# No gate product in the last period, and the last product's second bank summed and stored by halves of columns

## The chip, the cores and the metric

The kernel runs on one core of one Trainium2 chip. The time is device microseconds of one execution, lower is better. TensorE (PE) multiplies into PSUM banks of 128 partitions by 512 fp32 columns; VectorE (DVE) and ScalarE (ACT) take results out of the banks; SyncE (SP) and ACT issue DMA transfers.

## The reference

Linear attention without softmax, an RMS norm per head, and a gated feed-forward layer, all in fp32:

```python
kv  = np.einsum('bhsd,bhse->bhde', k, v)            # 8 batches, 8 heads, 576 rows, 64 columns
o   = np.einsum('bhsd,bhde->bhse', q, kv)
x   = o / np.sqrt(np.mean(o * o, axis=-1, keepdims=True) + 1e-6) * g_norm
x   = x.transpose(0, 2, 1, 3).reshape(8 * 576, 512)  # 4608 tokens of 512
h   = x @ w_in                                       # 512 -> 2048
g   = h * erf(np.maximum(h, 0) + np.log1p(np.exp(-np.abs(h))))   # h * erf(softplus(h))
out = g @ w_out                                      # 2048 -> 512
```

## The kernel before

The 4608 tokens are worked in nine groups of 512. Groups 0 to 7 are the first 512 rows of each batch; the ninth holds the 64 rows left over of each of the eight batches. Of the 2048 hidden columns, `BATCH` = 4 blocks of 128 form a batch of work, and `NB` = 4 batches make a group. The order of all instructions is written out by hand; there is no scheduler behind it.

From the third group on, each fp32 product is made of three fp32r products of parts ("forms") of its operands, which run at one pass each. `product` is the helper: it takes two PSUM banks, `n_ps` and `m_ps`, in turn from six; eight matmuls (two forms by four contraction blocks) sum into `n_ps`, four (the third form) into `m_ps`, all 512 columns wide. `hidden` uses it for h, `result` for the output: `result(T, b, j, g, w)` computes the 128 token rows j of group T, batch b, and adds the two banks into the sum `es[j]` in SBUF. For batches after the first of a group these are two VectorE operations of 128x512: `add_scaled` (L440) of `n_ps` times a constant, then `add` (L445) of `m_ps`.

The loop over periods m runs one step longer than there are batches. In period m the engines compute h of batch m (four calls of `hidden`), its softplus and erf on ACT, and the output of batch m - 1 (four calls of `result`, j = 0 to 3). After some of the calls of `result`, VectorE multiplies h by erf(softplus(h)) in two halves of the token columns, the "gates" (L876, 128x1024 each, `due_halves` says which). Before the next output product the gates are cut into forms: ACT takes the upper part (L405), VectorE the other two (L408, L411).

The last period, m = `batches` = 36, has no h to compute: it holds only the four output products of batch 35. Batch 35 is the fourth of the ninth group, so after each `result` the finished rows are stored. The lines that say which gates are due:

```python
            if m == batches - 1:
                due_halves = (j,) if j < 2 else ()
            else:
                due_halves = range(2) if j == (2 if to_last else 1) else ()
```

In period 36 these give both halves after j = 1. They multiply batch 35's h by its s once more; the forms of batch 35 were cut before, and nothing reads this h again.

`store` (L535) writes a block of the ninth group as two transfers of 64 rows by 512 columns, 128 KB each, one issued by SP and one by ACT, since the two halves of the partitions belong to two batches. At the end SP waits for all transfers and the engines meet in a closing barrier.

Of the kernel before, what the change touches and what calls it, by code (L numbers as in the profile page):

```python
# [60 lines left out]
def kernel(  # L61
# [13 lines left out]
    DM, DF = moe_w_in.shape[0], moe_w_in.shape[1] // 2  # L75
    J = 4
    G = J * P
    R = S - G
# [74 lines left out]
    for i in range(2):  # L153
        nc.gpsimd.dma_start(
            out=g_col[i * D : i * D + D, :], in_=g_norm.rearrange("(d one) -> d one", one=1)
# [100 lines left out]
    def weights():  # L256

        w_next("split")
        w_next("join")
        w_next("load")  # L260
# [178 lines left out]
    def add_scaled(out_, ps, scale):  # L439
        nc.vector.scalar_tensor_tensor(  # L440
            out=out_, in0=ps, scalar=scale, in1=out_, op0=ALU.mult, op1=ALU.add
        )

    def add(out_, ps):
        nc.vector.tensor_tensor(out=out_, in0=ps, in1=out_, op=ALU.add)  # L445

    banks = [(ps_h, "h"), (ps_h, "h")] + [(ps_o, f"o{i}") for i in range(4)]

    def product(weights, moving, turns=True):


        n_ps, m_ps = (
            pool.tile([P, G], FP32, name=name, tag=tag)
            for name, (pool, tag) in zip(("n_ps", "m_ps"), banks[:2])
        )
        if turns:
            banks.extend(banks[:2])
            del banks[:2]
        for ps, forms in ((n_ps, (0, 1)), (m_ps, (2,))):
            for k in range(4):  # L460
                for form in forms:
                    nc.tensor.matmul(  # L462
                        ps,
                        lhsT=weights(form, k),
                        rhs=moving(form, k),
                        start=(form == forms[0] and k == 0),
                        stop=(form == forms[-1] and k == 3),
                    )
        return n_ps, m_ps
# [36 lines left out]
    def hidden(T, f, turns=True):  # L506

        w = w_now["in", f].pop(0).rearrange("p i (c f) -> p i c f", c=KC).bitcast(FP32R)
        x = x_forms[T]
        return product(lambda form, c: w[:, form, c], lambda form, c: x[form][:, c], turns)  # L510
# [14 lines left out]
                stop=last,  # L525
            )

    def store(T, j, e):
        if T < B:
            rows = out[T * S : T * S + G, :].rearrange("(p j) f -> p j f", j=J)  # L530
            nc.sync.dma_start(out=rows[:, j, :], in_=e)
            return
        for h, side in enumerate((nc.sync, nc.scalar)):
            first_row = (2 * j + h) * S + G
            side.dma_start(out=out[first_row : first_row + R, :], in_=e[h * R : h * R + R, :])  # L535

    es = {}

# [10 lines left out]
    def unit(name):  # L549
        return gate.tile([P, G], FP32, name=name, tag=name[0])  # L550
# [30 lines left out]
    first_batch, batches = FIRST * NB, NG * NB  # L581
# [5 lines left out]
    def load_parts(which, n):  # L587


        pool = w_out_p if which == "out" and len(w_seq["out"]) > BATCH else w_in_p  # L590
        for _ in range(n):
            if w_seq[which]:
                key = w_seq[which].pop(0)
                t = pool.tile([P, 3, G], FP32, name=f"w_{which}_parts", tag="w")
                nc.sync.dma_start(out=t, in_=w_kept[key])
                w_now.setdefault(key, []).append(t)
# [47 lines left out]
    for n in range(FIRST * FC + 1):  # L644
        T, f = divmod(n, FC)
        if n == FC:
# [6 lines left out]
            forms = late.tile([P, 3, KC, G], FP32R, name="x_forms0")  # L653
# [24 lines left out]
        if T == FIRST - 1 and f >= WHOLE:  # L678
            n_ps, m_ps = hidden(T, f, turns=False)
        elif T < FIRST:  # L680
# [10 lines left out]
            for i, c in blocks:  # L691
# [3 lines left out]
                    rhs=xT[T][:, c, :],  # L695
# [3 lines left out]
        if T < FIRST:  # L699
            if n == whole:  # L700
                old_h = acc.tile([P, BATCH, G], FP32, name="h", tag="e")
            h = hs[n] = old_h[:, n - whole] if n >= whole else unit("h_sb")
# [28 lines left out]
        if n >= LAG:  # L731
            T2, f2 = divmod(n - LAG, FC)
# [21 lines left out]
    def part(h, half):  # L754
        return h[:, :, half * 2 * P : half * 2 * P + 2 * P]

    def cut_upper(h, half):

        t = late_r.tile([P, 3, BATCH, 2 * P], FP32R, name=f"g_forms{half}")
        upper(part(h, half), t[:, 0])  # L760
        return t

    def cut_lower(h, half, t):
        lower(part(h, half), *(t[:, i] for i in range(3)))

    def result(T, b, j, g, w):

        ps = product(
            lambda form, f: g[j // 2][:, form, f, j % 2 * P : j % 2 * P + P],
            lambda form, f: w[f][:, form],  # L770
        )
        if b == 0:
            if j == 0:
                all_e = wide.tile([P, J, DM], FP32, name="e", tag="a")
                es.update((i, all_e[:, i]) for i in range(J))
            nc.vector.tensor_scalar(
                out=es[j], in0=ps[0], scalar1=SHIFT - 1.0, scalar2=None, op0=ALU.mult
            )
        else:
            add_scaled(es[j], ps[0], SHIFT - 1.0)  # L780
        add(es[j], ps[1])


    FETCH = ("", "in", "in", "out", "in", "out", "in", "out out")
# [2 lines left out]
    for m in range(first_batch, batches + 1):  # L787
        T, b = divmod(m, NB)
        todo = []
        if T + 1 < NG:  # L790
            todo = list(attention(T + 1, b))
            if b == 0:
                side = late_r if T % 2 == FIRST % 2 else late
                forms = side.tile([P, 3, KC, G], FP32R, name=f"x_forms{(T + 1) % 2}")
                x_forms[T + 1] = [forms[:, i] for i in range(3)]

        def piece():
            if todo:
                todo.pop(0)()


        places = (0, 2, 3, 5, 6, 8)
        if T + 1 == B:
            places = (0, 0, 0, 5, 6, 7)
            if b == NB - 1:


                places, todo[3] = (0, 0, 0, 4, 6, 7), partial(todo[3], table=False)
                todo[5] = partial(chain, todo[5], softplus_table)
        elif b == NB - 1:  # L810
            places = (0, 2, 3, 5, 6, 7)

        def pieces(place):
            while todo and places[-len(todo)] <= place:
                todo.pop(0)()

        def fetch(place):
            for which in FETCH[place].split():
                load_parts(which, 1)


        to_last = m == B * NB - 1
        pieces(0)
        g, done = g_next, len(g_next)
        g_next = []
        if m < batches:

            pool, tag = (acc, "e") if m % 2 else (wide, "b")
            h = pool.tile([P, BATCH, G], FP32, name="h", tag=tag)
            s = gate_r.tile([P, BATCH, G], FP32, name="s", tag="s")  # L830
        for i in range(BATCH):
            if m < batches:
                n_ps, m_ps = hidden(T, b * BATCH + i)
            fetch(i)

            def evacuate():
                nc.scalar.activation(h[:, i], n_ps, AF.Copy, scale=SHIFT - 1.0)  # L837
                add(h[:, i], m_ps)


            early_copy = i == 0 and m == B * NB
            if early_copy:
                evacuate()
            if i == 0:
                for half in range(done, 2):
                    g.append(cut_upper(old_h, half))
            if done <= i < 2:
                cut_lower(old_h, i, g[i])
            if m < batches:
                if not early_copy:  # L850
                    evacuate()
                nc.scalar.activation(s[:, i], h[:, i], AF.Softplus)  # L852
            pieces(i + 1)
        if m < batches:
            for i in range(2):
                nc.scalar.activation(part(s, i), part(s, i), AF.Erf)  # L856
            if len(todo) < 2:
                softplus_table()
        T2, b2 = divmod(m - 1, NB)
        w = [w_now["out", b2 * BATCH + f].pop(0).bitcast(FP32R) for f in range(BATCH)]  # L860
        for j in range(J):
            result(T2, b2, j, g, w)
            fetch(BATCH + j)
            if b2 == NB - 1:
                store(T2, j, es.pop(j))
            if j == 1 and m == batches - 1:
                cut_lower(h, 0, g_next[0])

            if m == batches - 1:
                due_halves = (j,) if j < 2 else ()  # L870
            else:
                due_halves = range(2) if j == (2 if to_last else 1) else ()
            if to_last:
                pieces(BATCH + 1 + j)
            for half in due_halves:
                nc.vector.tensor_tensor(  # L876
                    out=part(h, half), in0=part(h, half), in1=part(s, half), op=ALU.mult
                )
            if j == 0 and m == batches - 1:
                g_next.append(cut_upper(h, 0))  # L880
            pieces(BATCH + 1 + j)
        old_h = h
# [33 lines left out]
```

## Time and profile before

| | |
|---|---|
| median of 4 runs | 944.36 us |
| the runs | 943.32, 944.28, 944.47, 944.45 us |
| profiled execution | 943.32 us, span 941.5 us (1.8 us lie around the span) |
| TensorE busy | 925.0 us, 98% of the span, granted clock 1.00 |
| VectorE busy | 742.9 us, 79% |
| ScalarE busy | 615.4 us, 65% |
| last matmul ends | 935.68 us |
| last VectorE sum ends | 937.75 us |

The span runs from the first to the last instruction of the program in the profiled execution. All positions in time below are microseconds from its start. "SPq" and "ACTq" rows are DMA issues by SP and ACT: how long the issuing takes, not the transfer. A busy matmul row counts a matmul from its start to its modelled end, and matmuls overlap: twelve of one product start 0.227 us apart, while each lasts 0.39 us.

### The profile page before, as it was taken

The page shows a single profiled execution, that of the slowest core. Times are in us where ns is not written, and L with a number is a line of the kernel's source. Part 1 is how long each engine was busy: PE and PEld are TensorE (multiplying, and loading weights), DVE is VectorE, ACT ScalarE, POOL GpSimd, SP SyncE. Part 2 cuts the span into 40 slices and gives each one's busy share as a digit, 9 for nine tenths or more (in the row PEclk, how much of TensorE's full clock was granted, in tenths as well). Part 3 has the DMA queues.
Part 4 walks back from the last instruction along what each step waited for, and adds up shares of the span by engine and source line. Part 5 has one row for each costly group of instructions (what it writes and reads, how often), then busy time and mean ns, then how long its engine had stood idle before and what let it go on. Part 6 is the DMA issues. An engine that isn't in the chain of part 4 may idle for free.

```text
span 941.5 us, 11743 instructions
## 1 busy us (share of the span) xinstructions
PE 925.0 (98%) x4272; PEld 683.4 (73%) x4272; DVE 742.9 (79%) x1056; ACT 615.4 (65%) x825; POOL 2.4 (0%) x10
## 2 busy tenths in 40 slices
PE   6999999999999999999999999999999999999997
PEld 4344445666688888888888888888888888888886
DVE  3999858887677787788778888888887777787667
ACT  4898876776766666666666666666666666665551
POOL 1000000000000000000000000000000000000000
PEclk9999999999999999999999999999999999999999
DMA  9876406899699998998899889988896779778871
GB/s 264 280 202 202 146 1 240 315 352 335 219 363 345 309 314 269 322 309 293 286 288 312 293 298 309 315 301 296 282 338 259 265 248 350 285 281 291 352 261 46
DMA packets 111842, 259.78 MB, mean 276 GB/s; under 512 B 43864, under 2 KB 69544, under 8 KB 111784
## 3 DMA queue, kind: packets, MB, share of 16 engines
q1 hardware_dynamic: 110152, 256.73, 79.0%
q10 hardware_dynamic: 1568, 2.29, 0.8%
q8 instruction: 34, 0.56, 0.2%
q14 instruction: 24, 0.20, 0.1%
q0 software_dynamic: 64, 0.00, 0.0%
HBM read 224.40 MB, written 34.60 MB: 275 GB/s over the span
## 4 chain that ended last, share of the span: by engine, by line
PE 95%; DVE 3%; DMA 1%; ACT 1%; issue 0%; DVEq 0%
PE n_ps L462 46%; PE m_ps L462 23%; PE o_ps L520 10%; PE h_ps L692 6%; PE se_ps L325 3%; PE kv_ps L297 2%; PE qt_ps L319 2%; PE ms_ps L351 1%; PE ms_ps L347 1%; PE ms_ps L346 1%; PE kv_ps L324 1%; DMA q_sb<-in_q_dram 1%; DMA v_sb<-in_v_dram 1%; PE kv_ps L305 0%; DVE xT L378 0%; DVE qT L369 0%
## 5 line engine op out<-in xcount | busy, mean ns | idle before, releaser
L462 PE MATMUL n_ps<-x_forms,w_in_parts 128*128 128x512 f32 x896 | 232.6, 401 | 0.1
L462 PE MATMUL n_ps<-w_out_parts,g_forms 128*128 128x512 f32 x928 | 231.3, 391 | 0.0
L462 PEld LDWEIGHTS n_ps<-w_out_parts,g_forms 128*128 128x128 f32 x928 | 174.2, 188 | 38.4 <-issue 1.7
L462 PEld LDWEIGHTS n_ps<-x_forms,w_in_parts 128*128 128x128 f32 x896 | 166.8, 188 | 43.1 <-issue 9.1
L852 ACT ACTIVATE s<-h 128x512 f32<-128x512 f32 x112 | 71.0, 634 | 179.2 <-DVE h L445 179.2
L445 DVE TENSOR_TENSOR h<-m_ps,h 128x512 f32<-128x512 f32 x116 | 79.8, 688 | 59.8 <-ACT h L837 43.8
L462 PE MATMUL m_ps<-w_out_parts,g_forms 128*128 128x512 f32 x464 | 124.2, 389 | 0.0
L462 PE MATMUL m_ps<-x_forms,w_in_parts 128*128 128x512 f32 x448 | 120.0, 389 | 0.0
L520 PE MATMUL o_ps<-w_out_sb,h_sb 128*128 128x512 f32 x224 | 100.8, 593 | 0.3 <-DVE h_sb L642 0.3
L462 PEld LDWEIGHTS m_ps<-w_out_parts,g_forms 128*128 128x128 f32 x464 | 87.1, 188 | 18.0
L462 PEld LDWEIGHTS m_ps<-x_forms,w_in_parts 128*128 128x128 f32 x448 | 84.1, 188 | 17.6
L445 DVE TENSOR_TENSOR e<-m_ps,e 128x512 f32<-128x512 f32 x116 | 80.3, 692 | 18.2 <-PE m_ps L462 10.9
L440 DVE SCALAR_TENSOR_TENSOR e<-n_ps,e 128x512 f32<-128x512 f32 x88 | 60.4, 686 | 38.9 <-PE n_ps L462 38.9
L520 PEld LDWEIGHTS o_ps<-w_out_sb,h_sb 128*128 128x128 f32 x224 | 42.3, 190 | 48.9 <-issue 46.6
L411 DVE SCALAR_TENSOR_TENSOR g_forms<-g_forms 128x1024 fp32r<-128x1024 f32 x58 | 71.1, 1226 | 2.0
L408 DVE TENSOR_TENSOR g_forms<-h,g_forms 128x1024 fp32r<-128x1024 f32 x58 | 70.6, 1218 | 1.7 <-ACT g_forms L405 1.4
L876 DVE TENSOR_TENSOR h<-h,s 128x1024 f32<-128x1024 f32 x58 | 68.3, 1218 | 0.7 <-ACT s L856 0.7
L837 ACT ACTIVATE h<-n_ps 128x512 f32<-128x512 f32 x112 | 65.4, 584 | 3.4 <-PE n_ps L462 3.4
L405 ACT ACTIVATE g_forms<-h 128x1024 fp32r<-128x1024 f32 x58 | 58.9, 1059 | 12.1 <-PE m_ps L462 8.7
L692 PE MATMUL h_ps<-xT,w_in_sb 128*128 128x512 f32 x144 | 64.8, 594 | 0.7 <-DVE w_in_sb L240 0.6
L106 ACT ACT_TABLE_LOAD x44 | 56.5, 1283 | 0.7
L856 ACT ACTIVATE s<-s 128x1024 f32<-128x1024 f32 x56 | 56.3, 1053 | 0.3
(98 smaller groups left out, 1014.0 us busy)
## 6 DMA issues: line engine op xcount, KB each, us to landing
w_out_parts<-w_out SPq DMA_DIRECT2D x116, 768.0 KB
w_in_parts<-w_in SPq DMA_DIRECT2D x112, 768.0 KB
w_in<-w_new SPq DMA_DIRECT2D x16, 768.0 KB
q_sb<-in_q_dram SPq DMA_DIRECT2D x32, 256.0 KB
w_raw<-in_moe_w_out_dram SPq DMA_DIRECT2D x8, 1024.0 KB
out_dram<-e SPq DMA_DIRECT2D x32, 256.0 KB
k_sb<-in_k_dram SPq DMA_DIRECT2D x28, 287.5 KB
v_sb<-in_v_dram SPq DMA_DIRECT2D x28, 287.5 KB
```

What stands on the lines that cost most here:

```text
L106: nc.scalar.preload_act_table_set("softplus")
L405: nc.scalar.activation(high, x, AF.Copy, scale=1.0 + 2.0**-13)
L408: nc.vector.tensor_tensor(out=low, in0=x, in1=high.bitcast(FP32), op=ALU.subtract)
L411: nc.vector.scalar_tensor_tensor(out=both, in0=low.bitcast(FP32), scalar=SHIFT, in1=high.bitcast(FP32), op0=ALU.mult, op1=ALU.add,)
L440: nc.vector.scalar_tensor_tensor(out=out_, in0=ps, scalar=scale, in1=out_, op0=ALU.mult, op1=ALU.add)
L445: nc.vector.tensor_tensor(out=out_, in0=ps, in1=out_, op=ALU.add)
L462: nc.tensor.matmul(ps, lhsT=weights(form, k), rhs=moving(form, k), start=(form == forms[0] and k == 0), stop=(form == forms[-1] and k == 3),)
L520: nc.tensor.matmul(o_ps[j], lhsT=g[:, j * P : j * P + P], rhs=w_out_sb[:, f, :], start=(f == 0), stop=last,)
L692: nc.tensor.matmul(plain[i], lhsT=w_in_sb[:, c, i % FC * P : i % FC * P + P], rhs=xT[T][:, c, :], start=(c == 0), stop=(c == KC - 1),)
L837: nc.scalar.activation(h[:, i], n_ps, AF.Copy, scale=SHIFT - 1.0)
L852: nc.scalar.activation(s[:, i], h[:, i], AF.Softplus)
L876: nc.vector.tensor_tensor(out=part(h, half), in0=part(h, half), in1=part(s, half), op=ALU.mult)
```

## The change

Three edits that act only in the last period. `due_halves` is empty there, so the two L876 products of period 36 are gone. In the last product (m = 36, j = 3) the `m_ps` bank is computed by column halves: four matmuls of 256 columns for the left half, then four for the right, where there were four of 512. Its sum into `es[3]` is made by two VectorE operations of 128x256, and after each the half is stored by its own pair of transfers, 64 rows by 256 columns, where one pair of 64 rows by 512 columns was issued after the whole sum. The `n_ps` bank and its `add_scaled` stay whole.

```diff
-    def product(weights, moving, turns=True):
+    def product(weights, moving, turns=True, cuts=1):
...
-        for ps, forms in ((n_ps, (0, 1)), (m_ps, (2,))):
+        spans = [slice(i * G // cuts, (i + 1) * G // cuts) for i in range(cuts)]
+        for ps, forms, cols in [(n_ps, (0, 1), slice(0, G))] + [(m_ps, (2,), x) for x in spans]:
             for k in range(4):
                 for form in forms:
                     nc.tensor.matmul(
-                        ps,
+                        ps[:, cols],
                         lhsT=weights(form, k),
-                        rhs=moving(form, k),
+                        rhs=moving(form, k)[:, cols],
                         start=(form == forms[0] and k == 0),
                         stop=(form == forms[-1] and k == 3),
                     )
...
-    def store(T, j, e):
+    def store(T, j, e, cols=slice(0, DM)):
...
-            side.dma_start(out=out[first_row : first_row + R, :], in_=e[h * R : h * R + R, :])
+            side.dma_start(
+                out=out[first_row : first_row + R, cols], in_=e[h * R : h * R + R, cols]
+            )
...
-    def result(T, b, j, g, w):
+    def result(T, b, j, g, w, cuts=1):
...
+            cuts=cuts,
...
-        add(es[j], ps[1])
+        for i in range(cuts):
+            cols = slice(i * DM // cuts, (i + 1) * DM // cuts)
+            add(es[j][:, cols], ps[1][:, cols])
+            if cuts > 1:
+                store(T, j, es[j], cols)
...
-            result(T2, b2, j, g, w)
+            cuts = 2 if m == batches and j == J - 1 else 1
+            result(T2, b2, j, g, w, cuts)
             fetch(BATCH + j)
             if b2 == NB - 1:
-                store(T2, j, es.pop(j))
+                e = es.pop(j)
+                if cuts == 1:
+                    store(T2, j, e)
...
-            if m == batches - 1:
-                due_halves = (j,) if j < 2 else ()
+            if m >= batches - 1:
+                due_halves = (j,) if j < 2 and m < batches else ()
```

## The prediction

> **What bounds the kernel.** I read the page first, then the chain that ended last over the final 40 us, then the last 10 us as a timeline, and last the windows after the last arithmetic. Part 1 of the page says who is scarce:
>
> ```profile
> PE 925.0 (98%) x4272; PEld 683.4 (73%) x4272; DVE 742.9 (79%) x1056; ACT 615.4 (65%) x825; POOL 2.4 (0%) x10
> ```
>
> TensorE is busy 98% of the span; no edit off its path can gain anything in the body. The instruction lists of the two programs are the same on every engine up to the last period but for line and buffer numbers, so only what follows TensorE's last matmul can change. The chain of waits, its last pieces (start, us, what):
>
> ```profile
> 932.95 1.81 PE n_ps L462 x8
> 934.76 0.92 PE m_ps L462 x4
> 935.68 0.68 DVE e L445
> 936.36 0.61 DVE e L440
> 936.97 0.03 issue
> 937.00 0.02 DVEq L445
> 937.02 0.04 issue
> 937.06 0.69 DVE e L445
> ```
>
> TensorE is done at 935.68, and three VectorE operations still stand behind it, one of them for the product before the last. VectorE is late, and the timeline of the period says why:
>
> ```profile
> 932.01 0.69 DVE L445 TENSOR_TENSOR e<-m_ps,e 128x512 f32<-128x512 f32 x1
> ...
> 932.62 2.35 DVE L876 TENSOR_TENSOR h<-h,s 128x1024 f32<-128x1024 f32 x2
> ...
> 932.79 1.98 PE L462 MATMUL n_ps<-w_out_parts,g_forms 128*128 128x512 f32 x8
> ...
> 934.60 1.07 PE L462 MATMUL m_ps<-w_out_parts,g_forms 128*128 128x512 f32 x4
> 934.88 0.68 DVE L440 SCALAR_TENSOR_TENSOR e<-n_ps,e 128x512 f32<-128x512 f32 x1
> 935.67 0.69 DVE L445 TENSOR_TENSOR e<-m_ps,e 128x512 f32<-128x512 f32 x1
> 936.28 0.68 DVE L440 SCALAR_TENSOR_TENSOR e<-n_ps,e 128x512 f32<-128x512 f32 x1
> 937.06 0.69 DVE L445 TENSOR_TENSOR e<-m_ps,e 128x512 f32<-128x512 f32 x1
> ```
>
> The two L876 products sit between the sums of j=1 and j=2; the first matmul group of j=2 ended at 932.05 (930.07 + 1.98), so L440 of j=2 starts 2.8 us after its bank was full. Nothing reads what L876 writes here. After the last sum the stores remain (timeline of SP, then windows: last two columns are the share of the DMA engines and GB/s):
>
> ```profile
> 937.78 0.47 SPq L535 DMA_DIRECT2D out_dram<-e  x1
> ```
>
> ```profile
> 938.50:939.00 0.50, 0.00 (x0) 0.00 (x0) 0.00 (x0) 0.00 (x0) 0.00 (x0) 1.00 0.30 82
> 939.00:939.50 0.50, 0.00 (x0) 0.00 (x0) 0.00 (x0) 0.00 (x0) 0.00 (x0) 1.00 1.02 197
> 939.50:940.00 0.50, 0.00 (x0) 0.00 (x0) 0.00 (x0) 0.00 (x0) 0.00 (x0) 1.00 0.79 283
> 940.00:940.50 0.50, 0.00 (x0) 0.00 (x0) 0.00 (x0) 0.00 (x0) 0.00 (x0) 1.00 0.01 0
> ```
>
> The trace's packet records sharpen these windows: the last store pair's packets run from 938.90 to 940.06, so 1.12 us from issue to first packet, 1.16 us of packets for 256 KB, and 1.47 us from the last packet to the span's end at 941.53 (landing, SP's waits, the closing barrier).
>
> **The products that go.** Two instructions of 1.22 us, both wholly on the path. Without them L440 of j=2 follows L445 of j=1 at VectorE's usual distance, 0.61 us (935.67 to 936.28): 932.01 + 0.61 = 932.62, when its bank is full. L445 follows 0.79 later (934.88 to 935.67): 933.41 to 934.10, and its store moves from 936.39 to 934.13, so its packets (1.12 later, 1.16 long) are gone by 936.4, before the next store's. What is late next is no longer VectorE's queue but the banks of j=3. Its first bank is full at 932.79 + 1.98 = 934.77, L440 starts 0.04 later (as elsewhere in the trace: bank full at 915.72, L440 at 915.76), 934.81, and L445 could start at 935.60; its own bank is full at 935.67, so it starts at 935.71. Ending at 936.40 in one piece instead of 937.75, it would gain 1.35 us. That is less than the 2.35 removed, because VectorE now waits for TensorE.
>
> **The halved matmuls.** Four matmuls of 512 columns, one per 0.227 us (four starts from 934.60), become eight of 256, each with its own weight load. If width sets the distance, eight take 8 x 0.113 = 0.91 us, as now: cost nothing. A weight load lasts 0.188 us in its row, which would seem to forbid 0.113; but loads overlap. Where this kernel has short matmuls (L324, L325), loads follow each other faster than they last:
>
> ```profile
> 654.07 0.42 PEld L324 LDWEIGHTS kv_ps<-qT_last,bd_kv 128*128 128x128 f32 x2
> 654.41 0.30 PEld L325 LDWEIGHTS se_ps<-qT,bd_kv 128*128 128x128 f32 x2
> ```
>
> Two loads of 0.19 in 0.30 us: 0.11 apart. That is nearest in shape, so I take 0.113 and a bank full at 935.67 again. Bounds: nothing to 0.91 us (if each matmul kept 0.227); a gain has no source, since the columns streamed are the same.
>
> **The halved sum.** In the changed program's list only the first half's sum waits for PE, and it waits for the count after all eight matmuls; the second waits for nothing. So the first half starts at 935.71, not after four matmuls. No 256-column sum is in the trace: 512 columns take 0.692, 1024 take 1.22, so the straight line gives 0.427, and the next instruction starts 0.08 before the end reported (0.692 against 0.61). Halves: 935.71 to 936.14 and 936.05 to 936.48, 0.08 later than the whole sum; by the 64-column copies (0.216 each, L326) at least 0.2 each, by the 512-column row at most 0.69, or 937.01.
>
> The Trainium skill's page PSUM — Partial Sum Buffer, section "PSUM bank collisions raise a hardware error", says that TensorE may not write a bank while another engine reads it, other columns included, so guards go by bank. It speaks against this cut: by it the first half waits as the list shows; without it the first half could start at 935.60, and the whole change would gain about 0.1 us more. No run here shows a collision.
>
> **The halved store.** Each queue now issues twice for j=3, and the second issue stands behind the first on SP and on ACT. First: 936.14 + 0.03 = 936.17 (the 0.03 from 937.75 to 937.78), lasting 0.47, to 936.64. Second: its sum was ready at 936.48, so the queue is what holds it, 936.70 with 0.06 for the semaphore wait ahead of it. That semaphore is one that a store of j=0 last used, issued at 931.33 and long landed, so the wait itself costs nothing. Packets start 1.12 after issue: 937.29 and 937.82. Packets of 1,024 bytes take 46 ns (median of 2,048 in the trace, loads), of 2,048 bytes 84 ns; a half pair then takes 1.16 x 46/84 = 0.64 us: 937.29 to 937.93, and the second, queued behind it, to 938.57. Bound above: a packet takes as long whatever its size, 2.32 us in all, to 939.61. Bound below: the second pair is not held and takes 0.5 us, to 938.32. I take 938.57, since the 46 ns is a row of the same size.
>
> The Trainium skill's page DMA: Bandwidth & Descriptors, section "Anatomy of one DMA — SWDGE (gpsimd) path", gives a transfer about 2.0 us plus its bytes at 436 GB/s (another issuing path than this one). By that an estimate for a whole pair is 2.60 us from 936.43, to 939.03, and for the second half pair 2.30 from 936.70, to 939.00: halving the store is worth nothing. The trace has 2.28 from issue to last packet for the whole pair.
>
> By the rows alone, one whole store from 936.43 would end its packets at 936.43 + 1.12 + 1.16 = 938.71; halves end them at 938.57, less one more semaphore wait of 0.06 in SP's closing sequence. The halves are worth 0.08 us, the removed products 1.35.
>
> **Sum.** Last packet 940.06 to 938.57 is 1.49, less 0.06: 1.43 us. The profiled execution took 943.32 (span 941.53 and 1.79 around it): 941.89. It was the fastest of four; against the median of 944.36 I predict 942.93. 0.2% of the time is 1.89 us, about what a measurement of this kernel can tell from no change.
>
> **Rivals.**
> (a) *Halves cost what wholes cost.* Packets keep their time: last packet 939.61, gain 940.06 - 939.61 - 0.06 = 0.39; or matmuls keep 0.227 us: everything 0.91 later, gain 0.52. About 943.9. For: SP's own packets in the final stores mostly take 0.15 to 0.17 us, twice the median of their size, so size is not all. Against: the load spacing of 0.11 and the 46 ns.
> (b) *Slower: the second store of a queue is held until the first has landed.* SP's wait for the last whole pair ended at 940.44, 0.38 us after the last packet and 2.66 after the issue. Two in series from 936.17 end before 940.44 only if each takes under 2.14 us. With 1.12 + 0.64 + 0.38 = 2.14 it is even; with 2.66 each, 941.49, 1.05 us slower, 945.4. Against: before, j=1's store issued at 932.73 while j=0's packets were still running.
> (c) *More in the tail than the profile shows.* Three of four runs were 1 us longer than the profiled one; if they spend it in the stretch that is cut, up to 2.4 us goes: 942.0.
>
> **How the numbers follow.** Forecast 0.72, (a) 0.16, (b) 0.05, (c) 0.07. The bounds of the forecast alone give gains of 1.0 to 1.7 us, 942.7 to 943.4. Runs of before lie up to 1.04 from their median, so a median of a few runs may be half a microsecond off; that, (a) and (c) give 942.0 to 944.3. Faster by over 0.2% needs 0.46 us more than the forecast: two fifths of its 0.72 through that scatter, plus (c), 0.36. Slower by over 0.2% is (b) with scatter, 0.06. The rest, 0.58, is within.
>
> **What would show it.** Right: L440 of j=2 at about 932.6, VectorE idle before the last L445 and released by PE m_ps, TensorE's end unmoved at 935.7, both half sums within 0.8 us after it, and a span near 940.1. Wrong: eight last matmuls lasting over 1.2 us in all, packets of the half pairs still running after 939.2, a second store issued after the first one's packets end, or any change of the times ahead of 932 us.

## The result and the profile after

| | before | after |
|---|---|---|
| median, all runs | 944.36 us (53 runs) | 943.10 us (33 runs) |
| ratio | | 0.9987, 95% interval 0.9982 to 0.9992 |
| span of the profiled execution | 941.53 us | 940.91 us |
| last product's first matmul to the span's end | 8.75 us | 7.48 us |
| TensorE's end to the span's end | 5.86 us | 4.55 us |

The change is 1.26 us faster, against 1.43 predicted (942.93). It is within 0.2% (1.89 us), and its interval, 0.8 to 1.7 us of gain, excludes no change. The profiled execution of one kernel below, "own banks again", ran at a granted clock of 0.657 and took 1340.54 us, so its trace is compared with no other.

In the profiled execution of after, the last product begins at 933.43 where it began at 932.79 before, though the instructions ahead of it are the same: the body of one execution differs from that of another by that much (two executions of one kernel, the uneven split below, begin it at 933.49 and 933.97). So the spans of two executions say little here, and the stretch from the first matmul of the last product (m = 36, j = 3) to the end of the span is compared instead: 941.53 - 932.79 = 8.75 and 940.91 - 933.43 = 7.48, from the unrounded records. It is 1.27 us shorter. That the medians say 1.26 is partly luck, since their interval is 0.9 us wide.

Part 1 of the page of after, for the count: TensorE four matmuls more, VectorE one instruction less (two products gone, one sum more).

```profile
PE 924.9 (98%) x4276; PEld 683.8 (73%) x4276; DVE 740.8 (79%) x1055; ACT 615.7 (65%) x825; POOL 2.4 (0%) x10
```

The timeline of the last period after the change (start, us, engine, line, output and inputs, sizes, count, and in brackets the idle time ahead with who ended it):

```profile
932.64 0.69 DVE L445 TENSOR_TENSOR e<-m_ps,e 128x512 f32<-128x512 f32 x1
...
933.25 0.68 DVE L440 SCALAR_TENSOR_TENSOR e<-n_ps,e 128x512 f32<-128x512 f32 x1
933.43 1.98 PE L463 MATMUL n_ps<-w_out_parts,g_forms 128*128 128x512 f32 x8
934.04 0.69 DVE L445 TENSOR_TENSOR e<-m_ps,e 128x512 f32<-128x512 f32 x1
...
935.25 1.11 PE L463 MATMUL m_ps<-w_out_parts,g_forms 128*128 128x256 f32 x8
935.45 0.69 DVE L440 SCALAR_TENSOR_TENSOR e<-n_ps,e 128x512 f32<-128x512 f32 x1 [0.71 <-PE n_ps L463]
936.40 0.76 DVE L445 TENSOR_TENSOR e<-m_ps,e 128x256 f32<-128x256 f32 x2 [0.26 <-PE m_ps L463]
```

The issues of the last two store pairs, one row for each queue (the time from the first issue's start to the second's end):

```profile
936.85 1.11 SPq L536 DMA_DIRECT2D out_dram<-e  x2
936.85 1.39 ACTq L536 DMA_DIRECT2D out_dram<-e  x2
```

L440 of j=2 now follows L445 of j=1 at 0.61 us, as predicted, and VectorE waits for TensorE twice, 0.71 us for the first bank of j=3 and 0.26 for the second. Before, it ran without a gap and TensorE had been done for 1.4 us when the last sum began. Both half sums together take 0.76 us and start 0.04 after the bank is full.

The windows after the last arithmetic show the packets of the two half pairs, the last of which ended at 939.37 by the packet records:

```profile
937.50:938.00 0.50, 0.00 (x0) 0.00 (x0) 0.00 (x0) 0.00 (x0) 0.00 (x0) 1.00 0.06 12
938.00:938.50 0.50, 0.00 (x0) 0.00 (x0) 0.00 (x0) 0.00 (x0) 0.00 (x0) 1.00 0.93 211
938.50:939.00 0.50, 0.00 (x0) 0.00 (x0) 0.00 (x0) 0.00 (x0) 0.00 (x0) 1.00 0.87 193
939.00:939.50 0.50, 0.00 (x0) 0.00 (x0) 0.00 (x0) 0.00 (x0) 0.00 (x0) 1.00 0.50 109
```

### The profile page after: what moved, and what is told of

The parts are those of the page before. It is cut to its first block, busy times and chain, and to the rows that moved or that the text cites. A ratio compares the mean times of both kernels' runs of the same rounds, so it can differ in the third digit from the quotient of the medians.

```text
span 940.9 us, 11755 instructions
## 1 busy us (share of the span) xinstructions
PE 924.9 (98%) x4276; PEld 683.8 (73%) x4276; DVE 740.8 (79%) x1055; ACT 615.7 (65%) x825; POOL 2.4 (0%) x10
## 4 chain that ended last, share of the span: by engine, by line
PE 94%; DVE 3%; DMA 2%; ACT 0%; SPq 0%; issue 0%; DVEq 0%
PE n_ps L463 46%; PE m_ps L463 23%; PE o_ps L521 10%; PE h_ps L695 6%; PE se_ps L325 3%; PE kv_ps L297 2%; PE qt_ps L319 2%; DMA w_raw<-in_moe_w_in_dram 1%; PE ms_ps L351 1%; DMA v_sb<-in_v_dram 1%; PE ms_ps L346 1%; PE ms_ps L347 1%; PE kv_ps L324 1%; PE kv_ps L305 0%; DVE xT L378 0%; DVE qT L369 0%
## 5 line engine op out<-in xcount | busy, mean ns | idle before, releaser
L445 DVE TENSOR_TENSOR h<-m_ps,h 128x512 f32<-128x512 f32 x116 | 79.8, 688 | 59.8 <-ACT h L845 43.8
L463 PE MATMUL m_ps<-w_out_parts,g_forms 128*128 128x512 f32 (+1 forms) x468 | 124.2, 388 | 0.0
L445 DVE TENSOR_TENSOR e<-m_ps,e 128x512 f32<-128x512 f32 (+1 forms) x117 | 80.3, 687 | 18.3 <-PE m_ps L463 11.2
L440 DVE SCALAR_TENSOR_TENSOR e<-n_ps,e 128x512 f32<-128x512 f32 x88 | 60.4, 686 | 39.6 <-PE n_ps L463 39.6
L887 DVE TENSOR_TENSOR h<-h,s 128x1024 f32<-128x1024 f32 x56 | 66.0, 1218 | 0.7 <-ACT s L864 0.7
```

Source lines behind the costliest of these rows:

```text
L440: nc.vector.scalar_tensor_tensor(out=out_, in0=ps, scalar=scale, in1=out_, op0=ALU.mult, op1=ALU.add)
L463: nc.tensor.matmul(ps[:, cols], lhsT=weights(form, k), rhs=moving(form, k)[:, cols], start=(form == forms[0] and k == 0), stop=(form == fo ...
L887: nc.vector.tensor_tensor(out=part(h, half), in0=part(h, half), in1=part(s, half), op=ALU.mult)
```

## The experiments

The theory to be tested: the whole gain is that of the two gate products, and the halves bring nothing, because both lie in one bank and the first half's sum waits for the bank's last matmul. The rivals: the halves carry a good part of the gain; or the halves cost something that the gate products pay for. Ten runs on three chips follow. The table gives for each kernel its median beside that of before on the same chip, the ratio of the two kernels' times as recorded (up to 0.0003 off the quotient of the two medians), and the time from the last product's first matmul to the span's end in its trace.

| kernel | median, before beside it (us) | ratio (95% interval) | last product to end (us) |
|---|---|---|---|
| before | | | 8.75 |
| the change | 943.10, 944.36 | 0.9987 (0.9982 to 0.9992) | 7.48 |
| gates only | 943.55, 944.57 | 0.9987 (0.9978 to 0.9996) | 7.38 |
| halves only | 944.66, 944.57 | 1.0002 (0.9993 to 1.0011) | 8.77 |
| whole matmuls | 943.01, 944.57 | 0.9983 (0.9974 to 0.9992) | 7.43 |
| own banks | 942.78, 944.57 | 0.9984 (0.9975 to 0.9992) | 6.97 |
| gates twice | 946.64, 944.49 | 1.0025 (1.0016 to 1.0033) | 10.99 |
| quarters | 944.45, 944.49 | 1.0001 (0.9992 to 1.0009) | 9.01 |
| own banks, 384 and 128 | 942.83, 944.49 | 0.9980 (0.9971 to 0.9989) | 7.15 |
| the change again | 943.38, 944.57 | 0.9988 (0.9979 to 0.9998) | 7.46 |
| own banks again | 942.74, 944.57 | 0.9983 (0.9974 to 0.9992) | no comparable trace |
| own banks, 384 and 128, again | 942.70, 944.57 | 0.9983 (0.9975 to 0.9992) | 7.16 |

The medians tell 1.3 us from nothing, but not 0.1 us from 0.5; the last column does, since it repeats to 0.02 us (the change twice: 7.48 and 7.46; the uneven split twice: 7.15 and 7.16). It is one execution each, so of differences of 0.05 us only those that a matching difference within the trace explains are read below.

**Gates only.** The kernel before with one line changed:

```diff
-            if m == batches - 1:
-                due_halves = (j,) if j < 2 else ()
+            if m >= batches - 1:
+                due_halves = (j,) if j < 2 and m < batches else ()
```

> The kernel before without the two gate products of the last period; the last product, its sum and its store stay whole. Theory (the removed products carry the gain, the halves are worth nothing): L445 of j=3 starts 0.04 us after the last bank is full, ends 0.69 later, last packets about 2.3 us after the store's issue; gain 1.3 us, ratio to before 0.9986, 943.05 us, no different from the full change. Rival 1 (the halves hide a part of the last store and carry half of the gain or more): gain at most 0.7 us, 943.7 us. Rival 2 (the halves cost something real): faster than the full change by 0.3 us or more, 942.75 us or less.

The ratio is that of the full change, 0.9987 in both. The times alone would not decide between the theory and rival 1: the median is 943.55, 1.02 us below before and near the 943.7 of rival 1, and the interval allows 0.4 to 2.1 us. The trace decides. The end of its timeline:

```profile
936.25 1.07 PE L462 MATMUL m_ps<-w_out_parts,g_forms 128*128 128x512 f32 x4
936.45 0.69 DVE L440 SCALAR_TENSOR_TENSOR e<-n_ps,e 128x512 f32<-128x512 f32 x1 [0.71 <-PE n_ps L462]
937.36 0.69 DVE L445 TENSOR_TENSOR e<-m_ps,e 128x512 f32<-128x512 f32 x1 [0.21 <-PE m_ps L462]
```

The last sum starts 0.04 after the matmuls end at 937.32, the last packet ends 2.28 us after the store's issue, and the stretch is 8.75 - 7.38 = 1.37 us shorter than before; the prediction had 1.35 for this edit. Rival 1, that the halves carry half of the gain, is out by the stretch; so is rival 2's 0.3 us (it is 0.10 shorter than the full change's).

**Halves only.** The full change with `due_halves` as it was before.

```diff
-            if m >= batches - 1:
-                due_halves = (j,) if j < 2 and m < batches else ()
+            if m == batches - 1:
+                due_halves = (j,) if j < 2 else ()
```

> The full change with the two gate products put back into the last period. Theory: VectorE is late again, L440 of j=3 starts 1.5 us after its bank is full, and the halves move the last packet by less than 0.1 us; ratio to before 1.000, 944.4 us within 0.3. Rival 1 (the halves carry half of the gain or more): 943.7 us or less. Rival 2 (the halves cost something real): 944.7 us or more.

No difference from before, in the times and in the stretch (8.77 against 8.75); the median, 944.66, could not have told this from rival 2's 944.7, the stretch can. The two products stand where they stood and the sum of j=3 starts 1.4 us after its bank is full:

```profile
935.65 2.35 DVE L887 TENSOR_TENSOR h<-h,s 128x1024 f32<-128x1024 f32 x2
...
937.64 1.11 PE L463 MATMUL m_ps<-w_out_parts,g_forms 128*128 128x256 f32 x8
937.92 0.68 DVE L440 SCALAR_TENSOR_TENSOR e<-n_ps,e 128x512 f32<-128x512 f32 x1
938.71 0.69 DVE L445 TENSOR_TENSOR e<-m_ps,e 128x512 f32<-128x512 f32 x1
939.32 0.68 DVE L440 SCALAR_TENSOR_TENSOR e<-n_ps,e 128x512 f32<-128x512 f32 x1
940.10 0.76 DVE L445 TENSOR_TENSOR e<-m_ps,e 128x256 f32<-128x256 f32 x2
```

**Whole matmuls.** The full change without the halving in `product`; sum and store stay by halves.

```diff
             lambda form, f: w[f][:, form],
-            cuts=cuts,
         )
```

> The full change, but the last bank is computed by four matmuls of 512 columns again; its sum and its store stay by halves. Theory (in the changed kernel's trace the eight narrow matmuls start 0.12 us apart where four wide ones start 0.227 apart, so eight cost 0.05 us more than four): last bank full 0.05 us sooner, 943.05 us, no measurable difference from the full change. Rival 2 (the halved matmuls are a real cost): 942.7 us or less.

The stretch is 0.05 us shorter than in the full change, as expected; the times cannot tell the two apart. So about half of what the halves cost is in the matmuls: the last product takes 2.92 us with the narrow ones and 2.88 without. The rest, 7.43 against 7.38 of gates only, is a balance of larger terms in the sum and the stores. The first store is issued 0.27 us sooner after the sum's start, and the last pair's packets end 0.33 sooner after their issue; but that issue is the second, 0.56 after the first, and from the last packet to the end it takes 0.08 longer.

**Gates twice.** The kernel before, with the two products of period 36 issued twice. Nothing reads what they write.

```diff
-            for half in due_halves:
+            for half in [*due_halves] * (2 if m == batches else 1):
```

> The kernel before with the two gate products of the last period issued twice (four products of 1.22 us; nothing reads what they write). Theory: they lie on the path, each further one moves L440 of j=2 and all behind it by its whole length, 1.17 us at VectorE's start-to-start distance: 2.35 us slower than before, ratio 1.0025, 946.7 us; so taking two away gains less (1.3) than adding two costs, because without them VectorE waits for TensorE. Rival (VectorE's queue has slack there and the gain of the change came from elsewhere): under 1 us slower, 945.3 us or less.

2.15 us slower by the medians, 2.25 by the stretch; 2.35 was expected, with products 1.17 us apart where the trace has them 1.13 apart. The four products run from 934.43 to 939.05, and the sum of j=2 follows:

```profile
934.43 4.62 DVE L876 TENSOR_TENSOR h<-h,s 128x1024 f32<-128x1024 f32 x4
...
936.42 1.07 PE L462 MATMUL m_ps<-w_out_parts,g_forms 128*128 128x512 f32 x4
938.97 0.68 DVE L440 SCALAR_TENSOR_TENSOR e<-n_ps,e 128x512 f32<-128x512 f32 x1
```

The added pair costs its own distance in VectorE's queue, 4.62 - 2.35 = 2.27 us; the removed pair gave 1.37. The place is the same; the difference of 0.9 us is VectorE's new wait for TensorE, 0.71 + 0.21 in gates only.

**Own banks.** The gates are gone, and the whole last product, both banks, is made by column halves in two bank pairs, the left pair's sums and store standing ahead of the right pair's.

```diff
+    def last_result(T, j, g, w):
+
+        for cols in LAST:
+            ps = product(
...
+                cols=cols,
+            )
+            add_scaled(es[j][:, cols], ps[0][:, cols], SHIFT - 1.0)
+            add(es[j][:, cols], ps[1][:, cols])
+            store(T, j, es[j], cols)
...
+    LAST = (slice(0, 256), slice(256, 512))
```

> No gate products in the last period, and the whole last product (both banks) by column halves, the left half and the right half in bank pairs of their own; each half is summed and stored as soon as its own pair is full. Theory (halves bring nothing in the changed kernel because both halves lie in one bank, so the first half's sum waits for the last matmul): here the left half's sum and store run under the right half's matmuls, and after TensorE's end remain one sum of 256 columns, one store pair of half rows and the closing: 4.55 us after TensorE's end become about 3.95, less about 0.1 us for 24 narrow matmuls instead of 8 wide and 8 narrow ones; 0.5 us faster than the full change, ratio to before 0.9982, 942.6 us. Rival (what remains after TensorE's end is fixed and does not shrink with the size of the last piece): as the full change or slower by the matmuls, 943.1 to 943.2 us.

The end of its timeline, with the left half's sum at 935.99, under the right half's matmuls:

```profile
935.21 0.64 PE L462 MATMUL m_ps<-w_out_parts,g_forms 128*128 128x256 f32 x4
...
935.69 1.12 PE L462 MATMUL n_ps<-w_out_parts,g_forms 128*128 128x256 f32 x8
935.99 0.42 DVE L445 TENSOR_TENSOR e<-m_ps,e 128x256 f32<-128x256 f32 x1
...
936.65 0.64 PE L462 MATMUL m_ps<-w_out_parts,g_forms 128*128 128x256 f32 x4
936.85 0.42 DVE L440 SCALAR_TENSOR_TENSOR e<-n_ps,e 128x256 f32<-128x256 f32 x1 [0.43 <-PE n_ps L462]
937.38 0.42 DVE L445 TENSOR_TENSOR e<-m_ps,e 128x256 f32<-128x256 f32 x1
```

TensorE ends at 937.29 and the span 3.94 us later, against the 3.95 expected; with 24 narrow matmuls the product takes 0.11 us longer than in the full change. The stretch is 0.51 us shorter than the full change's. By the trace, the 0.62 us saved (unrounded) behind TensorE's end are 0.56 for a second issue that no longer stands behind the first and 0.11 for the last pair's packets, less 0.05 for a sum that starts 0.09 instead of 0.04 after the bank is full. In the times the step is 0.64 us on the one chip that ran both (943.38 to 942.74, below), with intervals that overlap: seen in the trace, not settled by the times alone.

**Quarters.** The full change with `cuts = 4`.

> The full change with the last bank computed, summed and stored by quarters of 128 columns instead of halves. Theory (pieces of one bank cannot overlap with its matmuls, and each queue needs 0.5 to 0.55 us per issue): sixteen matmuls 0.12 us apart cost about 1.0 us more than eight; the fourth issue stands 1.65 us behind the first instead of 0.56 behind, while the last piece's packets shrink by about 0.35 us: 1.0 + 1.1 - 0.3 - 0.35 (smaller first sum 0.13, smaller packets) = about 1.5 us slower than the full change, 944.6 us, no faster than before. Rival (smaller pieces shorten the end): 943.0 us or less.

1.53 us longer than the full change in the stretch, and no faster than before. The sixteen matmuls take 0.8 us more, not the 1.0 expected, since they start 0.111 us apart; the first of the four sums still waits for the last of them; and the fourth issue stands 1.84 us (SP) and 2.12 (ACT) behind the first, not 1.65. So the expected 1.5 us came out partly by misses that offset each other. The matmuls and the sums:

```profile
935.44 1.90 PE L463 MATMUL m_ps<-w_out_parts,g_forms 128*128 128x128 f32 x16
935.64 0.69 DVE L440 SCALAR_TENSOR_TENSOR e<-n_ps,e 128x512 f32<-128x512 f32 x1 [0.71 <-PE n_ps L463]
937.38 0.88 DVE L445 TENSOR_TENSOR e<-m_ps,e 128x128 f32<-128x128 f32 x4 [1.04 <-PE m_ps L463]
```

**Own banks, 384 and 128 columns.** Own banks with an uneven split.

```diff
-    LAST = (slice(0, 256), slice(256, 512))
+    LAST = (slice(0, 384), slice(384, 512))
```

> As the last product by column halves in bank pairs of their own, but split 384 to 128 columns. Theory (a matmul needs about 0.12 us however narrow, because of its weight load): twelve matmuls of 128 columns cost as much as twelve of 256, so TensorE ends about 0.7 us later than with equal halves, while the sum (0.29 instead of 0.42) and the packets (512 bytes a row) give back 0.3 to 0.4: 0.3 to 0.4 us slower than equal halves. Rival (matmul time goes by columns alone): 0.3 to 0.4 us faster than equal halves.

After TensorE's end 3.59 us remain instead of 3.94, but the product takes 3.56 instead of 3.03. Net 0.18 us worse than equal halves, in the direction expected and half as large: TensorE's end is 0.53 us later, not 0.7, the matmuls of 128 columns starting 0.111 us apart rather than 0.120, while the 0.35 given back is as expected. The times do not separate the two splits.

**Three again, on one chip.**

> The full change once more, on one chip with the next two. Theory: ratio to before 0.9987, 1.26 us faster, the same as gates alone.

> The last product by equal column halves in bank pairs of their own once more, on one chip with the full change. Theory, from the traces: from the first matmul of the last product to the span's end 6.97 us, against 7.47 in the full change: 0.5 us faster than the full change, ratio to before 0.9982. Rival (the end is fixed): the same as the full change.

> The split of 384 to 128 columns once more, on one chip with the equal halves. Theory, from the traces (7.15 us from the first matmul of the last product to the span's end): 0.2 us slower than equal halves, 0.3 faster than the full change, both too little to tell apart by the times alone. Rival (narrow last piece wins): 0.3 us or more faster than equal halves.

The change repeats its gain (0.9988). Own banks and the uneven split are lowest, 942.74 and 942.70; between these two nothing can be said from the times, and their intervals overlap that of the change.

## Why the prediction was right

- **The signs it named.** The prediction's times are in the clock of before's execution; the body of after runs 0.65 us later. With that taken off, L440 of j=2 starts at 932.61, TensorE ends at 935.71, the last packet ends at 938.73 and the span at 940.26, against 932.6, 935.7, 938.57 (and not after 939.2) and 940.1; the half sums end 0.79 us after TensorE, and the eight matmuls last 1.11.
- **Only the end can move, and VectorE's queue sets it.** Right, and shown from both sides: taking the products away gives 1.37 us, putting them back takes it all (halves only, 8.77), adding a second pair costs 2.25.
- **Of 2.35 us removed, 1.35 comes back, because the banks of j=3 are late next.** Right: 1.37 in gates only, with VectorE released by PE n_ps and PE m_ps.
- **The first half's sum waits for the whole bank.** Right: it starts 0.04 us after the eighth matmul, in quarters after the sixteenth. It is a wait of the program: only the last matmul of the bank signals. The Trainium skill's page PSUM — Partial Sum Buffer, section "PSUM bank collisions raise a hardware error", says that a bank is not to be read while TensorE writes another part of it. These kernels keep to that by their waits, so no run shows what would happen otherwise. Own banks, where the left half does not share a bank with the right, starts its left sum 0.14 us after its last left matmul ends (935.85, sum at 935.99), 1.3 us before TensorE is done.
- **The halves are worth 0.08 us.** The sign was wrong: they cost 0.10 (7.38 to 7.48). Taken term by term from the last bank's first matmul: the bank is full 0.04 later than predicted (the narrow matmuls start 0.120 apart, not 0.113); the half sums took 0.42 each, as the straight line said; the second issue came 0.56 us after the first, not 0.53; and from that issue to its last packet it was 1.97 us, not 1.87. The closing took 1.54 against the 1.53 predicted. Together 0.17 us, against the 0.16 by which the forecast of 1.43 was too high.
- **The term that was sized worst** is the half pair's packets: 0.64 us predicted from the 46 ns of the loads' 1,024-byte packets, 0.76 measured (938.62 to 939.37). SP's packets halved with their size, 162 to 81 ns (medians), but ACT's went only from 84 to 73. So rival (a) held in a small part.
- **When the second pair's packets start** was right by luck: 1.21 us after its issue, against 1.23 predicted. The prediction had them queue behind the first pair's packets, to the end of those. But the first pair's packets ran until 938.71 and SP's second began at 938.62, 0.18 us after SP's first had ended at 938.43. What holds them is the issue: SP's first packet came 0.65 to 0.67 us after the end of its issue in the last pair of every trace at full clock, whether a pair ran ahead or not, and the second issue lasts 0.55 us instead of 0.47.
- **Rival (b)**, a second store held until the first has landed, is out: its issue at 937.41 came before the first pair's packets began at 937.97, and its packets began at 938.62, before SP's wait for the first store ended at 938.89. **Rival (c)** did not come: no more than the profile's stretch was gained.
- **What the halved store saves.** The Trainium skill's page DMA: Bandwidth & Descriptors, section "Anatomy of one DMA — SWDGE (gpsimd) path", gives a fixed cost per transfer, for another issuing path, and counts the completion into it. The prediction set that against the last packet; to the end of SP's wait it was 2.66 us for the whole pair before and 2.36 for the second half pair, where the estimates from the page were 2.60 and 2.30. To the last packet a whole pair took 2.28 us and the second half pair 1.97, 0.31 less; the page's rule makes that 0.30, the scaling of packets made it 0.41. But the 1.97 contains the longer second issue: in own banks, where the issue stands alone, a half pair took 1.85, 0.43 less. There the scaling (1.12 + 0.64 = 1.76, 0.52 less) misses by 0.09 and the page's rule by 0.13, so neither is shown to be the better guide.

## What to carry to other kernels

At the end of a kernel whose main engine is full, list what the evacuating engine still has queued when the main engine stops, and first remove what nobody reads; the gain is that work less the wait that takes its place. Cutting the last piece helped here only where the pieces could overlap: in one bank the first piece's sum waited for the bank's last matmul, in banks of their own it did not (0.51 us). Each further cut cost a queue issue of half a microsecond where issues stood directly behind each other, and matmuls that hardly shrink with their width (0.120 us apart at 256 columns, 0.111 at 128). Where executions of one kernel differ by a microsecond in the body, compare a stretch of the trace that starts at the same instruction.

## What the runs showed of the hardware

- Distance of back-to-back fp32r matmuls, each with its own 128x128 weight load: 0.227 us at 512 columns, 0.176 at 384, 0.120 at 256, 0.111 at 128. Below 256 columns width hardly counts; a weight load is recorded as 0.19 us all along, but the loads of the 128-column matmuls follow each other at 0.11 (quarters).
- A store issued right behind another on the same queue takes longer to issue: SP 0.55 us instead of 0.47, ACT 0.79 instead of 0.50 (the change); of the four in quarters ACT's second took 0.78, its third and fourth 0.56. In own banks, where the issues stand 1.39 us apart, the last took 0.47 and 0.50. The first store of the period also took 0.56 and 0.57 (before), with none close ahead, so standing behind another is not the only cause.
- From the issue of an SP and ACT pair, with no issue directly ahead, to its last packet: 2.28 us at 512 columns (256 KB), 1.85 at 256, 1.69 at 128 (before, own banks, uneven split). A quarter of the bytes saves a quarter of the time.
- Of two stores issued together on SP and ACT, the one whose issue ended first had its packets first, in all 54 pairs of the last period in the eleven traces at full clock, though the two issues ended as little as 0.003 us apart. In the whole pairs the packets of the first took 0.162 to 0.171 us each (medians) and those of the other 0.084. In before, SP's ran in the last pair from 938.90 to 939.74 and ACT's from 939.52 to 940.07, while in the pair of j=1 ACT's were first.
